# Third tiles of an attention and FFN kernel in Strassen pairs, with the attention pieces re-placed around them

## The chip, the cores and the metric

The kernel runs on one NeuronCore of a Trainium2 chip. The metric is the time of one execution on the device in microseconds; of the kernel before three executions are shown (242.56, 241.81 and 242.93 us) and their median, 242.56 us, is the time before.

The core has five instruction streams that run at once and meet at semaphores. TensorE (PE in the profile) multiplies matrices into PSUM. VectorE (DVE), ScalarE (ACT) and GpSimd (POOL) work on elements. SyncE (SP) mostly issues transfers. Each stream runs in the order in which the program was written, so an instruction that waits holds up all that stand behind it on its engine.

## The reference, cut to what matters

Attention over 4 batches, 8 heads, 768 positions and head dimension 64 is followed by a gated FFN over all 3072 tokens.

```python
scores = scale * np.matmul(q, k.transpose(0, 1, 3, 2))
keep = is_global | is_local            # first 8 positions, or the last 96
scores = np.where(keep, scores - slopes * dist, -1e9)
a = softmax(scores)
x = np.matmul(a, v)                    # heads side by side: [3072, 512]
out = (np.maximum(x @ w_gate, 0) * (x @ w_val)) @ w_out      # 512 -> 1536 -> 512
```

Keys that count are a band of 96 positions and the 8 global ones, so scores are needed in narrow spans only.

## The kernel before

**Halves and stages.** The work is cut into eight halves of a batch (`NHALF`), 384 tokens each. Half c passes through attention, which leaves a normalised and transposed `xT` of 4 chunks of 128 by 384, and then through the FFN. The main loop (L834 on) runs one stage per half c from 2 to 7: the FFN of half c, with the attention of half c + 1 and the preparation of q and k of half c + 2 strewn among it. Halves 0 and 1 and the first weights are handled by an order written out by hand before the loop. In this text stage c begins at the first gate matmul of half c.

**FFN of a half** (`ffn_pieces`, L509). For each of 12 blocks of 128 hidden columns, `gate` (L521) does four matmuls of 384 columns into a PSUM bank and a relu on ScalarE; `val` (L528) does four more and a product on VectorE that reads the bank and writes the block of `ht`. Then `ht` (1536 hidden values by 384 tokens) is multiplied with `w_out`. The 384 tokens are three tiles of 128. A plain tile (`outp`, L533) is 12 matmuls of 512 columns in four parts of three, a copy on ScalarE and a store. From half 1 on, tiles 0 and 1 go as a pair by Strassen's scheme: hidden index, output columns and token tiles are each split in two, and seven products `p1` to `p7` (L595 to L629, via `block` at L579) of six matmuls with 256 columns replace eight. The sums of weight blocks (`bs`) are made once, at L805. The sums of `ht` blocks are made on VectorE for each half: `sum_cb`, `sum_ad`, `sum_de` (L566 to L576), parts of them right behind some val blocks (`behind`), three parts after the last. p1, p3 and p4 are copied from PSUM by ScalarE; p2 and p5 are each read by two VectorE combinations, p6 and p7 by one each, and p6 and p7 add onto the banks in which p3 and p1 were made, which are so held from p3 and p1 to the end. The order on TensorE is p4, p3, p1, p2, p5, p6, p7, after the plain third tile.

**Attention of a half** (`attention_pieces`, L493) is 26 small pieces over four pairs of heads. Each pair has three QK pieces (`piece_qk`, L408: the first makes the scores of both steps in four PSUM banks and the exps of step 0, the second the exps of step 1 and the masks of step 0, the third the masks of step 1), two AV pieces (`piece_av`, L416: value matmuls, ln on ScalarE, and at the second also the reciprocal by exp) and a norm (`piece_norm`, L443: two VectorE products, which write `xT`). The masks (`masks`, L349) multiply the exps by a table `m_all` of decays, one instruction per span: step 0 of an odd half has three spans (432, 144 and 96 elements), of an even half two (432 and 48).

**Preparation** (`early_pieces`, L377): eight casts of q and k on POOL, three DMA transposes on SP, and four pieces that bring the keys into order (`piece_order`, L372; copies into `kT` on POOL).

**The order.** `spread` (L659) gives pieces places as shares of a stage, `weave` (L664) puts each piece behind the first FFN item that reaches its place. An FFN item counts 0.65 per block or product, so a stage counts 22.75: 15.6 of gate and val blocks, 2.6 of the plain tile and 4.55 of products. Attention is spread over 0 to 0.8 (0.07 to 0.82 in stage 2), preparation over 0.25 to 0.75. A half's loads are issued at a stage's start.

**PSUM.** In the loop three banks (`ff`) serve gate, val, the plain tile and p4, p3, p1, p6, p7, and five (`x`) scores, AV, p2 and p5. A new tile takes a bank that is free or becomes free first in the planner's order, and waits for the last reader of the tile before.

**SBUF** pools that matter: `setupp` and `efp` close with the early part, and the pools of the late part (`late`, `osb` with three buffers for output rows, `sums`) are laid in their place. `dd` is the table of distances from which the masks are made.

Of the kernel before, what the change touches and what calls it, by code (L numbers as in the profile page):

```python
# [8 lines left out]
FP32 = mybir.dt.float32  # L9
BF16 = mybir.dt.bfloat16  # L10
AF = mybir.ActivationFunctionType
ALU = mybir.AluOpType
# [3 lines left out]
def kernel(  # L16
# [12 lines left out]
    nc = tc.nc  # L29
# [67 lines left out]
    dd = const.tile([128, 2, NN, WQ], BF16)  # L97
# [75 lines left out]
    kq0 = firstp.tile([128, 2, H, NN * D], FP32, name="kq0")  # L173
    kq1 = setupp.tile([128, 2, H, NN * D], BF16, name="kq1")
# [173 lines left out]

    def masks(s, p, g, steps=steps_of):  # L349
        for j in steps[s % 2][g]:  # L350
# [157 lines left out]

    def ffn_pieces(c):  # L509
# [43 lines left out]

        N2, D2 = N_FC // 2, DM // 2
        tiles_ = [slice(n * 128, (n + 1) * 128) for n in range(2)]

        def sums_of(name, *shape):
            if name not in st:
                st[name] = late["sums"].tile([128, *shape], BF16, name=name)
            return st[name]  # L560

        cb = lambda: sums_of("cb", N2, 2, 128)
        ad = lambda: sums_of("ad", N2, 128)
        de = lambda: sums_of("de", N_FC, 128)

        def sum_cb(i0, i1):  # L566
            nc.vector.tensor_tensor(cb()[:, i0:i1].rearrange("f i n t -> f i (n t)"), ht[:, i0:i1, 0:256],
                                    ht[:, N2 + i0 : N2 + i1, 0:256], op=ALU.add)

        def sum_ad(i0, i1):  # L570
            nc.vector.tensor_tensor(ad()[:, i0:i1], ht[:, i0:i1, tiles_[0]],
                                    ht[:, N2 + i0 : N2 + i1, tiles_[1]], op=ALU.add)

        def sum_de(i0, i1):
            x, y = (1, 0) if i0 < N2 else (0, 1)
            nc.vector.tensor_tensor(de()[:, i0:i1], ht[:, i0:i1, tiles_[x]], ht[:, i0:i1, tiles_[y]],  # L576
                                    op=ALU.subtract)

        def block(key, pool, left, right, start, stop):  # L579
            if start:  # L580
                st[key] = psum[pool].tile([128, 512], FP32, name=f"{pool}_ps")
            for i in range(N2):
                nc.tensor.matmul(st[key][:, 0:D2], lhsT=left(i), rhs=right(i),  # L583
                                 start=start and i == 0, stop=stop and i == N2 - 1,
                                 skip_group_check=not start)
            return st[key][:, 0:D2]

        c0, c1 = slice(0, D2), slice(D2, DM)
        bs = lambda name: lambda i: late["bs"][name][:, i]
        V2 = nc.vector.tensor_tensor  # L590

        def store(n, cols, eng=nc.sync):
            eng.dma_start(out=out_v[c, n][:, cols], in_=st["r", n][:, cols])

        def p4():  # L595
            for n in range(2):
                st["r", n] = late["osb"].tile([128, DM], FP32, name="osb")
            ps = block("d", "ff", lambda i: ht[:, N2 + i, tiles_[1]], bs("b21-b11"), True, True)
            nc.scalar.copy(st["r", 0][:, c0], ps)

        def p3():
            ps = block("c", "ff", lambda i: ht[:, i, tiles_[0]], bs("b12-b22"), True, True)
            nc.scalar.copy(st["r", 0][:, c1], ps)

        def p1():
            ps = block("a", "ff", lambda i: ad()[:, i], bs("b11+b22"), True, True)
            nc.scalar.copy(st["r", 1][:, c1], ps)
# [6 lines left out]
        def p5():  # L614
# [3 lines left out]
            if c == NHALF - 1:  # L618
                store(1, c0)
                store(0, c1)  # L620
# [258 lines left out]
```

## Time and profile before

| what | value |
|---|---|
| median of three executions | 242.56 us |
| the profiled execution | 241.74 us |
| its span, first to last instruction | 239.9 us |
| mean granted TensorE clock | 0.998 |
| TensorE busy | 233.5 us, 97% |
| VectorE busy | 173.3 us, 72% |
| ScalarE busy | 153.4 us, 64% |
| GpSimd busy | 85.9 us, 36% |
| stages 3, 4, 5, 6 | 26.91, 27.67, 27.02, 27.47 us |
| stage 7, to the last combination's start | 22.8 us |

How to read it: the span is what the program's instructions cover; the execution's own time is 1.8 us longer. A matmul's listed duration reaches past the start of the next one, so the cost of a run of matmuls is taken from start to start; the same holds, with a tenth of a microsecond, on VectorE and ScalarE. An idle time in brackets carries the engine whose signal came last. Idle time on an engine that nobody waits for costs nothing.

### The profile page before, as it was taken

To read this page: it belongs to the slowest core of one execution; us is meant where nothing else is said; L and a number is where in the kernel's file an instruction comes from. 1 tells how busy PE (TensorE), PEld (TensorE's weight loads), DVE (VectorE), ACT (ScalarE), POOL (GpSimd) and SP (SyncE) were. 2 spreads that over 40 slices of the span, in tenths; PEclk is the share of its full clock that TensorE was granted. 3 is DMA by queue.
4 is the path that set the end of the run, shared out by engine and by line. 5 is a ranking of instruction groups with operands and counts; after the bars stand their busy time and mean duration, and the time that the engine had idled before them with its cause. 6 is when DMAs were issued, how large, how long until landed. Compare 5 with 4: busy or idle time off the path is not lost.

```text
span 239.9 us, 5355 instructions
## 1 busy us (share of the span) xinstructions
PE 233.5 (97%) x1937; PEld 146.6 (61%) x1945; DVE 173.3 (72%) x456; ACT 153.4 (64%) x347; POOL 85.9 (36%) x202
## 2 busy tenths in 40 slices
PE   7899999999999999999999999999999999999994
PEld 3655555665458566666668566676658566676663
DVE  7775955869677788777787687866887677764643
ACT  5897883337775777748774777638774677733330
POOL 6767893208414860903274060902350000000000
PEclk9999999999999999999999999999999999999999
DMA  6999999993976997098519939398431200030003
GB/s 200 181 198 177 257 234 219 185 162 61 270 178 134 301 150 131 8 185 257 108 25 122 285 93 133 19 166 262 67 68 44 90 0 0 3 129 3 4 27 104
DMA packets 69603, 31.42 MB, mean 131 GB/s; under 512 B 47160, under 2 KB 66616, under 8 KB 69576
## 3 DMA queue, kind: packets, MB, share of 16 engines
q0 software_dynamic: 31744, 8.71, 35.3%
q1 hardware_dynamic: 36616, 21.45, 35.1%
q10 hardware_dynamic: 1216, 0.92, 1.2%
q8 instruction: 15, 0.25, 0.4%
q14 instruction: 12, 0.10, 0.1%
HBM read 28.41 MB, written 6.29 MB: 145 GB/s over the span
## 4 chain that ended last, share of the span: by engine, by line
PE 91%; ACT 3%; DVE 2%; issue 1%; ACTq 0%
PE ff_ps L518 53%; PE ff_ps L538 9%; PE ff_ps L583 8%; PE x_ps L427 6%; PE x_ps L397 4%; PE x_ps L583 3%; PE t_ps L459 2%; PE s_ps L341 2%; PE t_ps L272 1%; PE t_ps L682 1%; ACT lnd L436 1%; PE t_ps L310 1%; DVE xT L446 1%; PE s_ps L321 1%; ACT rcp L441 0%
## 5 line engine op out<-in xcount | busy, mean ns | idle before, releaser
L518 PE MATMUL ff_ps<-xT,wg 128*128 128x384 bf16 x384 | 80.7, 326 | 0.5 <-ACT grelu L525 0.4
L518 PE MATMUL ff_ps<-xT,wv 128*128 128x384 bf16 x384 | 80.2, 326 | 0.0
L531 DVE TENSOR_TENSOR ht<-ff_ps,grelu 128x384 bf16<-128x384 f32 x96 | 53.1, 554 | 28.5 <-PE ff_ps L518 13.8
L525 ACT ACTIVATE grelu<-ff_ps 128x384 bf16<-128x384 f32 x96 | 47.1, 492 | 39.4 <-PE ff_ps L518 20.9
L518 PEld LDWEIGHTS <-wg 128*128 128x128 bf16 x384 | 35.9, 98 | 23.9 <-issue 0.9
L518 PEld LDWEIGHTS <-wv 128*128 128x128 bf16 x384 | 36.1, 97 | 23.4 <-issue 1.2
L406 ACT ACTIVATE es<-x_ps 128x360 bf16<-128x360 f32 (+2 forms) x96 | 36.8, 444 | 16.9 <-PE x_ps L397 16.8
L359 DVE TENSOR_TENSOR es<-es,m_all 128x432 bf16<-128x432 bf16 (+4 forms) x108 | 31.2, 334 | 8.2 <-ACT es L406 7.8
L446 DVE TENSOR_TENSOR xT<-x_ps,rcp 64x384 bf16<-64x384 f32 x48 | 26.6, 554 | 9.4 <-ACT rcp L441 8.8
L436 ACT ACTIVATE lnd<-x_ps 64x384 f32<-64x384 f32 x48 | 23.3, 485 | 12.5 <-PE x_ps L427 11.8
L538 PE MATMUL ff_ps<-wo_sb,ht 128*128 128x512 bf16 x112 | 29.6, 379 | 0.4
L363 POOL CAST kqc<-ks 128x384 bf16<-128x384 f32 x24 | 11.6, 532 | 32.3 <-DMA ks<-in_k_dram 32.3
L137 POOL DMA_DIRECT2D vbuf<-in_v_dram x25 | 21.6, 880 | 2.6 <-DMA wv<-in_moe_w_val_dram 2.1
L427 PE MATMUL x_ps<-es,vbuf 128*128 128x216 bf16 (+4 forms) x216 | 21.8, 225 | 0.0
L427 PEld LDWEIGHTS <-vbuf 128*128 128x128 bf16 x216 | 15.8, 97 | 7.7
L538 PEld LDWEIGHTS <-ht 128*128 128x128 bf16 x120 | 10.8, 97 | 9.8 <-issue 0.2
L263 POOL COPY kT<-kqT 128x240 bf16<-128x240 bf16 x16 | 6.9, 430 | 23.0 <-DMA kqT<-kqc 20.5
L363 POOL CAST kqc<-qs 128x384 bf16<-128x384 f32 x24 | 11.6, 522 | 8.1 <-DMA qs<-in_q_dram 8.1
L259 POOL COPY kT<-kqT 128x360 bf16<-128x360 bf16 x10 | 6.0, 604 | 19.9 <-DMA kqT<-kqc 19.9
L441 ACT ACTIVATE rcp<-lnd 128x384 f32<-128x384 f32 x24 | 12.6, 524 | 0.7
L347 ACT ACTIVATE ef<-s_ps 128x720 bf16<-128x720 f32 (+2 forms) x16 | 10.9, 710 | 2.1 <-PE s_ps L341 1.8
L397 PE MATMUL x_ps<-kqT,kT 64*128 64x216 bf16 (+4 forms) x216 | 11.8, 224 | 0.2
(115 smaller groups left out, 252.8 us busy)
## 6 DMA issues: line engine op xcount, KB each, us to landing
out_dram<-osb SPq DMA_DIRECT2D x22, 256.0 KB, 2.7
ks<-in_k_dram SPq DMA_DIRECT2D x6, 768.0 KB, 5.5
qs<-in_q_dram SPq DMA_DIRECT2D x6, 768.0 KB, 12.1
vbuf<-in_v_dram POOLq DMA_DIRECT2D x21, 120.0 KB, 7.9
wg<-in_moe_w_gate_dram POOLq DMA_DIRECT2D x3, 512.0 KB, 7.9
wv<-in_moe_w_val_dram POOLq DMA_DIRECT2D x3, 512.0 KB, 9.8
wo_sb<-in_moe_w_out_dram POOLq DMA_DIRECT2D x1, 1536.0 KB, 19.6
kq<-in_q_dram ACTq DMA_DIRECT2D x2, 192.0 KB, 4.7
```

What stands on the lines that cost most here:

```text
L137: nc.gpsimd.dma_start(out=v_dst(b, NG + r0, NG + r0 + n, j), in_=v[b, :, KT * j + r0 : KT * j + r0 + n, :].rearrange("h p d -> p h d"))
L359: nc.vector.tensor_mul(for_all, for_all, mk)
L363: nc.gpsimd.tensor_copy(kqc[:, :, i].rearrange("t n (h d) -> t h n d", d=D)[:, 2 * p : 2 * p + 2], of[s][:, 2 * p : 2 * p + 2, :].rearrang ...
L406: nc.scalar.activation(es[:, e, 0:c], banks[e][:, 0:c], AF.Exp, bias=0.0, scale=scale)
L427: nc.tensor.matmul(av3[:, :, a : a + w], lhsT=vb[:, j, z0 : z0 + 128], rhs=es[:, e, c : c + NN * w].rearrange("k (n p) -> k n p", n=NN), s ...
L436: nc.scalar.activation(ln[o0 : o0 + 64], av[d0 : d0 + 64, 0:QH], AF.Ln, bias=0.0, scale=1.0)
L446: nc.vector.tensor_tensor(xT_of[s][r, p, :], av_of[s, p, e][r, 0:QH], av_of[s, p, "r"][r], op=ALU.mult)
L518: nc.tensor.matmul(st[key][:, 0:QH], lhsT=w_of(w, dc, fc), rhs=xT_of[c][:, dc, :], start=(dc == 0), stop=(dc == N_DC - 1))
L525: nc.scalar.activation(gr, psg[:, 0:QH], AF.Relu, bias=0.0, scale=1.0)
L531: nc.vector.tensor_tensor(ht[:, fc, :], psv[:, 0:QH], st["gr", fc], op=ALU.mult)
L538: nc.tensor.matmul(ps2, lhsT=ht[:, fc, n * 128 : (n + 1) * 128], rhs=wo_sb[:, fc, :], start=(fc == 0), stop=(fc == N_FC - 1))
L583: nc.tensor.matmul(st[key][:, 0:D2], lhsT=left(i), rhs=right(i), start=start and i == 0, stop=stop and i == N2 - 1, skip_group_check=not s ...
```

## The change

Four things are changed together.

1. In halves 4 and 5, and in 6 and 7 (`PAIRED`), the two third tiles no longer go as plain tiles: half 5 multiplies its own third tile and that of half 4 as a second Strassen pair (`products3`), and half 7 those of 7 and 6. The Strassen code becomes a function `strassen` of any two tiles. Halves 4 and 6 so have only their own pair behind the last val block, with p3 ahead of p4 and p4 in an `x` bank (`bare`); halves 5 and 7 have two pairs in a row. `ht` of the earlier half is kept until the pair is done. The sums of the second pair are made in halves 5 and 7, three behind val blocks 1, 6 and 7 and two after the last.
2. The first three attention pieces (scores, exps and masks of the first pair of heads) of halves 5 and 7 move a stage forward, to between the products of halves 3 and 5 (places 0.82 to 0.93 and 0.885 to 0.975).
3. In stages 4 and 6 the last AV piece and the last norms have fixed places (0.76 and 0.84), behind the last val block and behind the sums and p1; the other pieces are spread over 0.07 to 0.735.
4. The masks of step 0, for halves from 3 on, are copied once on POOL into a table without gaps (`pack_mask`, five copies, between the casts and the ordering copies of half 2), and one VectorE instruction per pair of heads uses them instead of three or two.

Beside these, output rows have four buffers instead of three, and `dd` moves to the pool of the early part.

```diff
-    dd = const.tile([128, 2, NN, WQ], BF16)
+    dd = setupp.tile([128, 2, NN, WQ], BF16, name="dd")
...
+    def pack_mask(half, i):
+        todo = [by[half, j] for j in steps_later[half][0]]
+        if half not in packed_of:
+            packed_of[half] = late["packed"].tile([128, H, sum(NN * t[2] for t in todo)], BF16, name=f"packed{half}")
+        c = sum(NN * t[2] for t in todo[:i])
+        j, _, w, m = todo[i]
+        nc.gpsimd.tensor_copy(
+            packed_of[half][:, :, c : c + NN * w].rearrange("k h (n t) -> k h n t", n=NN),
+            m_all[:, :, 0 if j == 0 else 1, :, m : m + w])
...
     def masks(s, p, g, steps=steps_of):
+        if s > 2 and g == 0:
+            mk = packed_of[s % 2][:, 2 * p : 2 * p + 2]
+            es = es_of[s, p, steps[s % 2][0][0]][0][:, :, 0 : mk.shape[2]]
+            nc.vector.tensor_mul(es, es, mk)
+            return
...
+    def strassen(pair, sums, bare=False):
...
+        def p4():
+            ps = block("d", "x" if bare else "ff", lambda i: h(1, N2 + i, N2 + i + 1)[:, 0], bs("b21-b11"), True, True)
+            nc.scalar.copy(rows(0)[:, c0], ps)
...
+        return sum_cb, sum_cb_of, sum_ad, sum_de, [(0.65, f) for f in (((p3, p4) if bare else (p4, p3)) + (p1, p2, p5, p6, p7))]
...
+    PAIRED = (4, 6)
+    third_of = {}
...
+        plain = range(NN) if c < 1 else () if c - c % 2 in PAIRED else (NN - 1,)
+        sum_cb, _, sum_ad, sum_de, products = strassen([(c, ht, 0), (c, ht, 1)], "sums", c in PAIRED)
...
+        rest = (lambda: sum_ad(3, 6), lambda: sum_cb(3, 6), lambda: sum_de(9, 12))
+        if c in PAIRED:
+            third_of[c] = ht
+        elif c - 1 in PAIRED:
+            _, cb3, ad3, de3, products3 = strassen([(c, ht, NN - 1), (c - 1, third_of[c - 1], NN - 1)], "sums3")
+            behind[1] = [lambda: cb3(1)]
+            behind[6] = [lambda: ad3(0, N_FC // 2)]
+            behind[7] = [lambda: de3(0, N_FC // 2)]
+            rest = (lambda: cb3(0), lambda: de3(N_FC // 2, N_FC)) + rest
...
+            f2 += (products3 if c - 1 in PAIRED else []) + products
+            places = (2, 3, 5) if plain else (0, 1, 2) if c in PAIRED else (0, 1, 2, 3, 4)
+            for at, f in list(zip(places, rest))[::-1]:
                 f2.insert(at, (0.0, f))
...
-    late["osb"] = ctx.enter_context(tc.tile_pool(name="osb", bufs=3, reuse_waits="tile"))
+    late["osb"] = ctx.enter_context(tc.tile_pool(name="osb", bufs=4, reuse_waits="tile"))
...
+    packs = [lambda half=half, i=i: pack_mask(half, i) for half, i in ((1, 0), (1, 1), (1, 2), (0, 0), (0, 1))]
...
-              casts[7], *xs, lambda: spread_v_globals(1), *order_k[:2]):
+              casts[7], *xs, lambda: spread_v_globals(1), *packs, *order_k[:2]):
...
+        if c + 1 < NHALF:
+            pieces = ahead.pop(c + 1, None) or attention_pieces(c + 1)
+            if c in PAIRED:
+                placed.append([(0.76, pieces[-2][1]), (0.84, pieces[-1][1])])
+                placed.append(spread(pieces[:-2], 0.07, 0.735))
+            else:
+                placed.append(spread(pieces, *(0.07, 0.82) if c == 2 else (0.0, 0.8)))
+        if c + 1 in PAIRED:
+            ahead[c + 2] = attention_pieces(c + 2)
+            placed.append(spread([ahead[c + 2].pop(0) for _ in range(3)], *(0.885, 0.975) if c - 1 in PAIRED else (0.82, 0.93)))
```

The seven products and their combinations are those of the code before, with tile 0 and tile 1 replaced by the two tiles of the pair (`h(0, ...)` and `h(1, ...)`). With the changed counts stages 4 and 6 count 20.15 items' worth and stages 5 and 7 24.7.

## The prediction

> **What bounds the kernel now.** I read the page first: engine shares and the chain that ended last.
>
> ```profile
> span 239.9 us, 5355 instructions
> PE 233.5 (97%) x1937; PEld 146.6 (61%) x1945; DVE 173.3 (72%) x456; ACT 153.4 (64%) x347; POOL 85.9 (36%) x202
> PE 91%; ACT 3%; DVE 2%; issue 1%; ACTq 0%
> ```
>
> TensorE is busy for 97% of the span and 91% of the last chain is its own. So a change is worth the TensorE time it removes, less the new waits. Then I cut the trace into stages, one per half c, at the first gate matmul of each (start:end length, then busy time per engine).
>
> ```profile
> 104.78:131.69 26.91, 26.86 (x214) 17.45 (x214) 20.01 (x51) 18.34 (x44) 11.28 (x25) 1.00 0.71 134
> 131.69:159.36 27.67, 27.56 (x232) 17.85 (x230) 21.47 (x54) 18.98 (x44) 9.93 (x23) 1.00 0.72 132
> 159.36:186.38 27.02, 26.97 (x214) 17.45 (x214) 20.56 (x50) 18.34 (x44) 7.26 (x20) 1.00 0.47 118
> 186.38:213.85 27.47, 27.40 (x232) 17.84 (x231) 20.41 (x54) 18.98 (x44) 0.00 (x0) 1.00 0.08 30
> ```
>
> These are stages 3 to 6. TensorE has under 0.2 us of idle time in each; VectorE has 6 to 7 us, but not everywhere. Third, the timeline of the last stage prices both ways to multiply a tile: the plain third tile, then p4 and p3, then p1.
>
> ```profile
> 229.28 2.75 PE L538 MATMUL ff_ps<-wo_sb,ht 128*128 128x512 bf16 x11
> 231.88 1.47 PE L583 MATMUL ff_ps<-bs,ht 128*128 128x256 bf16 x12
> 233.19 0.82 PE L583 MATMUL ff_ps<-bs,ad 128*128 128x256 bf16 x6
> ```
>
> Start to start, the plain tile's 12 matmuls (one record is missing) take 2.60 us, 217 ns each, and 12 products' matmuls 1.31 us, 109 ns each. Last, VectorE at the end of stage 5: two sums, the last norms, a sum, the first combination.
>
> ```profile
> 181.02 0.36 DVE L571 TENSOR_TENSOR ad<-ht 128x384 bf16<-128x384 bf16 x1
> 181.30 0.55 DVE L567 TENSOR_TENSOR cb<-ht 128x768 bf16<-128x768 bf16 x1
> 182.25 1.12 DVE L446 TENSOR_TENSOR xT<-x_ps,rcp 64x384 bf16<-64x384 f32 x2 [0.41 <-ACT rcp L441]
> 183.39 0.36 DVE L576 TENSOR_TENSOR de<-ht 128x384 bf16<-128x384 bf16 x1
> 184.51 0.42 DVE L611 TENSOR_TENSOR osb<-x_ps,osb 128x256 f32<-128x256 f32 x1 [0.76 <-ACT osb L607]
> ```
>
> Prices, start to start: a sum of 384 elements 0.28, of 768 0.48, a pair of norms 1.14, a combination 0.33 (184.51, 184.85, 185.18). A val product takes 0.59 when the next instruction reads it (174.60 to 175.19).
>
> **The change, part by part.**
>
> *The pairs.* Each removes two plain tiles, 2 x 2.60 = 5.20 us, and adds 42 matmuls of 256 columns, 42 x 0.1093 = 4.59. That is 0.61 a pair, **-1.22 us** for two, all on TensorE. A rule speaks against this. The Trainium skill ("TensorE: Matmul & The Clock Gate", Back-to-back issue gap) gives sustained spacings of about 81 ns at 128 columns and 131 ns at 512; interpolated, an estimate of 98 ns at 256, and a pair would cost 42 x 0.098 - 24 x 0.131 = 1.0 us more instead of 0.6 less, +1.9 for both. The rows show 217 and 109, nearly proportional to columns, and decide.
>
> On VectorE stages 5 and 7 gain five sums of 768 elements (2.4 us) and six combinations (2.0 us). On ScalarE three copies of 0.37 replace two of 0.57, 0.0 net. ScalarE has 8 us idle per stage. Stage 7 has no attention; its VectorE is busy 12.1 of 26 us, so the extra work is covered.
>
> *Masks packed.* An odd half's first mask step is now 432+144+96 elements in three instructions, 0.56 us (133.78 to 134.34). One of 672, between the sums of 384 and 768, is 0.42: 0.14 x 4 off VectorE per odd half, some 0.1 x 4 per even half. TensorE doesn't wait on it except for one attention block: five value matmuls at 152.51 held it 0.50 instead of 0.30, four at 179.68 0.39 instead of 0.28. In the new order these blocks lie further behind their masks: **-0.3**, bounds -0.3 and 0.
>
> *Packing copies.* Five copies on POOL, 4608 elements. The copies of kT give 0.36 us between starts for 240 elements and 0.48 for 360, so 1.0 ns an element and 0.12 fixed: 5.2 us, put between the last cast and the first ordering copy.
>
> ```profile
> 47.17 0.50 POOL L363 CAST kqc<-qs 128x384 bf16<-128x384 f32 x1
> 54.78 0.74 POOL L259 COPY kT<-kqT 128x360 bf16<-128x360 bf16 x1 [7.12 <-DMA kqT<-kqc]
> ```
>
> POOL waits there for 7.12 us for the transposes, so I cost the copies at nothing. Behind them on POOL's queue are the keys of half 2 (needed by TensorE at 57.23, there at 55.96, 1.3 us of slack), the markers that let SP load half 3's q and k (57.2), and half 3's v; its first keys are in order at 76.4, its scores come at 79.19. Without the cover they'd cost the excess over 8.4 us. The other side: masks beside a POOL copy took 0.93 instead of 0.60 (151.96). At that half speed the wo sum at 51.38 ends 0.6 late and the val product behind it at 53.0; its PSUM bank is wanted at 53.23. So 0. The Trainium skill ("SBUF — State Buffer", SBUF: two separate sides) says that a GpSimd instruction and a VectorE one with two SBUF inputs exclude each other for a whole instruction. Then that sum would wait until about 52.5 and TensorE would lose an estimated 0.4 us (a sum of +0.5 instead of +0.1). The row's slowdown of half is milder.
>
> *Earlier scores.* They add no work: 0.51 us of TensorE moves from stage 4 into 3, and from 6 into 5. At 134.0 and 188.69 TensorE waits 0.19 and 0.18 for a relu behind the first exps; with these gone from there, **-0.37**, bounds -0.4 and 0. Half 5's keys are ordered by 124.75, wanted at 128.3; half 7's have 5 us. Half 6's come within the shorter stage 4: in order at 150.4, wanted about 158. No DMA is moved; on SP's queue the three stores of a half become two in halves 4 and 6 and four in 5 and 7, still behind the half's transposes and ahead of the next loads.
>
> *dd in the early pool, a fourth osb buffer:* space only, 0. dd's last reader (the masks) ends some 20 us before that space is reused.
>
> *New waits, end of stage 3.* p3 ends at 128.25; scores to 128.76; p7 then ends at 132.04. ScalarE's four exps delay p1's copy to 130.0 and the second exps to 130.8. VectorE: p2's combinations 130.3 to 131.0, masks to 131.5, p5's to 132.17, p6's to 132.55. The next stage's first val product takes p6's bank and is due at 132.37: **+0.25** with a restart. Bounds 0 to 0.5.
>
> *End of stages 4 and 6.* No plain tile follows val 11 (zero at its end on TensorE). The attention pieces crowd: AV of pair 2 puts its ln and rcp ahead of relu 10 on ScalarE, so VectorE runs val 10 1.0 before zero, then a sum and norms (1.14), and val 11 only at 1.05 to 1.61. p4 starts at 0.96 and its sixth matmul wants val 11 at 1.5: 0.15. The sums end at 2.66, the last norms, put behind them, at 3.80; then six combinations, p6's ending at 5.56, while the next stage's first val is due at 5.37: 0.25. **+0.4 each**, bounds 0 to 0.8.
>
> *End of stage 5*, zero as before. VectorE's queue: val 11 at 0.27, then 0.59, sums 0.48 and 0.48, masks 0.57, sum 0.28, norms 1.14, sum 0.48, two combinations 0.67, sum 0.28, two 0.67 and the pair's p6 0.33, at 6.24; last norms 1.14; its p7 at 7.75. TensorE: three attention blocks of 0.28 and seven products of 0.655 end at 5.43, p4 of the next pair at 6.08. Its p3 wants the bank of the first pair's p6, at 6.30: 0.25. Its p1 gets p4's bank, which ScalarE frees at 6.7, and doesn't wait. After p2 the scores of half 7 take four of five x banks and p2 holds the fifth, so p5, ready 0.51 after p2, waits until an exp or two combinations free one, 0.95 after it: 0.45, with p6, p7 and the next stage's gate queued behind it on TensorE. Then masks and combinations queue into stage 6: 0.2. **+0.9**, bounds 0.45 (the x bank; no reason removes it) to 1.7 (p1 must take the first p7's bank, at 7.8).
>
> *Sum:* -1.22 -0.30 -0.37 +0.25 +0.40 +0.90 +0.40 = **+0.06 us**. The profiled execution took 241.74 (span 239.9 and 1.8 around it), 0.82 below the median of 242.56 that the change is compared with. So 242.56 + 0.06: **242.6**, no difference: 0.5% (1.2 us) is about what a measurement of this kernel can tell from no change.
>
> **The rivals.**
>
> *The waits don't come* (faster). If VectorE catches up in the tails, as before (it idles 0.76 ahead of the first combination at 184.51), only the x bank's 0.45 is left: -1.89 + 0.45 = -1.44, **241.1**. For it: bounds of 0 in three places. Against it: the removed 2.60 us covered just these sums, and stage 5's queue fills 7.5 us with no gap.
>
> *VectorE bounds stage 5's end* (slower, near the bound). p1 waits until 7.8: +0.8, and the stage-6 end takes its upper bound, +0.4 more: **243.8**. For it: three ff banks, of which two are held for whole pairs. Against it: p4's bank is free 1.1 us earlier.
>
> *POOL's packing runs over* (slower). In the trace, beside dense VectorE work, the kT copy of 360 took 0.74 and 0.86: 1.9 to 2.25 ns an element, 9.4 to 11.0 us for all five. From 47.67 that ends at 57.1 to 58.7, the first keys 1.2 later, and TensorE stands 1.1 to 2.7: with the sum, **244.6** at 2.0. It decides from 8.4 us of copying on. Against it: between 47.7 and 51.4 VectorE does only val products, 0.56 in each 1.3 us.
>
> **How the numbers follow.** No difference 0.47, waits don't come 0.25, VectorE bounds 0.18, packing 0.10. Faster: 0.25 and 0.02 of the forecast's lower edge, 0.27. Slower: 0.10, half of 0.18 and 0.03 of the upper edge, 0.22. Same: 0.51. The forecast's own range is 241.6 to 243.6 (its bounds together, as independent errors). For 8 in 10 it reaches to the faster rival, 241.0, and past the VectorE rival, 244.0; left out are the packing case and half a tenth on either side.
>
> **What would show it.** Right: no 512-column matmuls in stages 4 to 7, 84 more of 256 columns at 109 ns; stage 3 27.7 us, stage 4 24.5, stage 5 30.2, stage 6 24.5, stage 7 24.8 to its last matmul (22.8 before); POOL's five copies 5 to 7 us before 54.8; TensorE idle ahead of half 7's p5. Wrong: TensorE gapless at these stage ends, or late ahead of 57.23, or products slower than 109 ns.

## The result, and the profile after

The changed kernel takes 243.22 us (median of 14 runs, 242.74 to 244.57), the kernel before, run beside it, 241.76 us (14 runs, 240.86 to 242.93). The ratio is 1.0072, with a 95% interval of 1.0056 to 1.0088: 1.7 us slower (1.46 between the two medians). The predicted 242.6 us and its range hold the time, but the forecast behind them, no difference, does not stand: by the 0.5% named there this is a slowdown. That the time came within 0.6 of 242.6 is in part luck. The prediction counted from 242.56, the median of three executions, and 14 executions put the kernel before at 241.76. Counted from there, its +0.06 would have given 241.8.

The profiled execution of the changed kernel took 244.09 us, of which 242.3 are the span; it is 0.87 above the median. The page answers to the lines shown of before:

```profile
span 242.3 us, 5435 instructions
PE 233.5 (96%) x1977; PEld 149.9 (62%) x1981; DVE 182.1 (75%) x446; ACT 153.2 (63%) x349; POOL 92.4 (38%) x207
PE 81%; DVE 9%; ACT 4%; issue 3%; DMA 1%; ACTq 0%; DVEq 0%
```

VectorE (DVE) is busy 8.8 us longer (173.3 before), GpSimd (POOL) 6.5. In the chain that ended last TensorE's share falls from 91% to 81% and VectorE's rises from 2% to 9%: TensorE now waits for VectorE. The same stages as before, 3 to 7, from one first gate matmul to the next (start:end length, then PE, PEld, DVE, ACT, POOL busy; the prediction cut the stages of before one matmul later, 0.16 to 0.17 us, which leaves their lengths as they are to 0.01):

```profile
106.08:133.51 27.43, 27.38 (x226) 17.64 (x225) 20.69 (x49) 19.77 (x48) 11.46 (x25) 1.00 0.73 135
133.51:158.43 24.92, 24.64 (x211) 16.27 (x208) 19.83 (x43) 16.88 (x39) 10.00 (x23) 1.00 0.52 124
158.43:189.53 31.10, 29.80 (x257) 20.64 (x255) 25.34 (x61) 20.29 (x50) 8.70 (x21) 1.00 0.55 120
189.53:213.86 24.33, 24.33 (x210) 16.36 (x208) 19.12 (x46) 16.88 (x39) 0.00 (x0) 1.00 0.06 23
213.86:238.87 25.01, 24.93 (x182) 17.50 (x179) 16.57 (x39) 8.11 (x18) 0.00 (x0) 1.00 0.13 48
```

Compare length and PE busy in each row: the difference is TensorE's idle time, 0.28 us in stage 4 and 1.30 in stage 5, where it was 0.11 and 0.05. The wait for a stage's first val product lies behind the cut, so it counts in the next stage. Cut in this way, the prediction's terms and the profiles give (us; the last stage to the end of its last matmul, not counting how far its listed time reaches past the next start):

| stage | 3 | 4 | 5 | 6 | 7 | sum |
|---|---|---|---|---|---|---|
| before | 26.92 | 27.67 | 27.02 | 27.47 | 22.77 | 131.85 |
| predicted | 27.43 | 24.57 | 30.37 | 24.53 | 25.01 | 131.91 |
| after | 27.43 | 24.92 | 31.10 | 24.33 | 25.01 | 132.79 |

The row "predicted" is worked out afterwards from the terms. The prediction's own list, 27.7, 24.5, 30.2, 24.5 and 24.8, counts the wait at the end of stage 3 in stage 3 and is rounder elsewhere. By the row, stages 3 and 7 came as predicted; stage 4 is 0.35 too long, stage 5 0.73, stage 6 0.20 shorter. That makes the 0.9 us which these stages lose. The rest lies ahead of stage 3, which begins at 106.08 instead of 104.61: 1.47 us in the profiled executions. The two profiles are level up to the first sum of w_out's quarters (51.37 and 51.38 us), so this is lost behind it. The profiled execution is 0.87 above its median, so this second loss may be smaller in most executions. There are two losses to explain.

**Ahead of stage 3: the packing.** From the timeline of the changed kernel (start, length, engine, line; idle time before and what ended it in brackets):

```profile
49.07 4.54 POOL L358 COPY packed<-m_all 128x1728 bf16<-128x1728 bf16 x5
...
50.89 0.56 DVE L649 TENSOR_TENSOR ht<-ff_ps,grelu 128x384 bf16<-128x384 f32 x1 [0.74 <-PE ff_ps L636]
...
51.37 2.65 DVE L862 TENSOR_TENSOR bs<-wo_sb 128x768 bf16<-128x768 bf16 x1
...
53.94 0.55 DVE L649 TENSOR_TENSOR ht<-ff_ps,grelu 128x384 bf16<-128x384 f32 x1
54.40 0.54 DVE L862 TENSOR_TENSOR bs<-wo_sb 128x768 bf16<-128x768 bf16 x1
54.53 0.32 PE L636 MATMUL ff_ps<-xT,wg 128*128 128x384 bf16 x1 [1.15 <-DVE ht L649]
```

The five packing copies run back to back from 49.07 to 53.61. VectorE's sum of w_out's quarters (L862) starts at 51.37 and takes 2.65 us, where it takes 0.54 at 54.40: it ends 0.4 after the last copy. The val product queued behind it starts at 53.94, and TensorE, whose PSUM bank that product frees, stands for 1.15 us. The val product at 50.89, which reads PSUM, ran beside the same copies in its usual 0.56.

**Stage 4's end: the key copies.** The same view, at the end of stage 4:

```profile
152.48 0.53 POOL L259 COPY kT<-kqT 128x360 bf16<-128x360 bf16 x1 [6.14 <-DMA kqT<-kqc]
152.52 0.71 DVE L564 TENSOR_TENSOR de<-ht 128x384 bf16<-128x384 bf16 x1
...
154.29 0.56 DVE L649 TENSOR_TENSOR ht<-ff_ps,grelu 128x384 bf16<-128x384 f32 x1
...
154.91 0.28 PE L570 MATMUL x_ps<-bs,ht 128*128 128x256 bf16 x1 [0.22 <-DVE ht L649]
154.99 0.66 POOL L259 COPY kT<-kqT 128x360 bf16<-128x360 bf16 x1
...
155.18 0.89 DVE L553 TENSOR_TENSOR cb<-ht 128x768 bf16<-128x768 bf16 x1
...
155.60 0.53 POOL L260 COPY kT<-kqT 128x24 bf16<-128x24 bf16 x1
...
155.99 0.35 DVE L564 TENSOR_TENSOR de<-ht 128x384 bf16<-128x384 bf16 x1
...
159.23 0.48 PE L636 MATMUL ff_ps<-xT,wv 128*128 128x384 bf16 x2 [0.32 <-DVE osb L613]
```

A sum of 384 elements took 0.71 at 152.52 and 0.35 at 155.99; one of 768 took 0.89, and 0.55 elsewhere. The long ones lie beside the copies that put half 6's keys in order, and the two engines take turns: the sum at 155.18 ends 0.42 after the copy of 154.99 does (155.65), and the copy of 24 elements at 155.60, 0.20 where it stands alone, ends when the sum does, to 0.06. In the kernel before the same copies began at 149.48, 17.95 us into the stage, and met masks (0.93 for 0.60) and one sum (0.55 for 0.35) that no product was held up by. They begin when the transposed keys land, 18.97 us into the changed stage; that stage is 2.75 us shorter, so they now meet the sums that its products wait for. Val 11 comes late for the sixth matmul of p4 (p1 starts 0.39 us late by it), the sum of 768 late for p2 (0.12), and the combinations late for the next stage's val product.

**Stage 5's end.** VectorE and TensorE from the same view:

```profile
179.73 0.84 DVE L377 TENSOR_TENSOR es<-es,m_all 128x432 bf16<-128x432 bf16 x2
...
184.18 0.42 DVE L613 TENSOR_TENSOR osb<-ff_ps,osb 128x256 f32<-128x256 f32 x1
...
184.65 0.81 PE L570 MATMUL ff_ps<-bs,ht 128*128 128x256 bf16 x6 [0.60 <-DVE osb L613]
185.30 0.82 PE L570 MATMUL ff_ps<-bs,ad 128*128 128x256 bf16 x6
...
187.56 0.81 PE L570 MATMUL x_ps<-wo_sb,cb 128*128 128x256 bf16 x6 [0.38 <-ACT es L424]
```

The masks at 179.73 took 0.84, beside the ordering of half 7's keys (177.7 to 181.7 on GpSimd): 0.76 to the next instruction, where 0.57 was predicted. The sums on either side of them hold VectorE 0.07 longer each, and p6's combination, at 184.18, ends 6.77 after the last gate and val products (177.83) where 6.24 was predicted. The second pair's p3 waits 0.60 for that bank, 0.77 with the restart, instead of 0.25. p1 (185.30) follows without a wait. p5 waits 0.38 for an x bank, 0.44 with the restart, as predicted.

### The profile page after: what moved, and what is told of

It reads as the page before. It is cut to its first block, busy times and chain, and to the rows that moved or that the text cites. A ratio compares the mean times of both kernels' runs of the same rounds, so it can differ in the third digit from the quotient of the medians.

```text
span 242.3 us, 5435 instructions
## 1 busy us (share of the span) xinstructions
PE 233.5 (96%) x1977; PEld 149.9 (62%) x1981; DVE 182.1 (75%) x446; ACT 153.2 (63%) x349; POOL 92.4 (38%) x207
## 4 chain that ended last, share of the span: by engine, by line
PE 81%; DVE 9%; ACT 4%; issue 3%; DMA 1%; ACTq 0%; DVEq 0%
PE ff_ps L636 51%; PE ff_ps L570 7%; PE x_ps L445 5%; PE ff_ps L656 5%; PE x_ps L415 4%; PE x_ps L570 3%; DVE xT L464 2%; PE t_ps L477 2%; PE s_ps L341 2%; PE t_ps L272 2%; ACT lnd L454 1%; PE t_ps L733 1%; PE t_ps L310 1%; DMA out_dram<-osb 1%; DVE ht L649 1%
## 5 line engine op out<-in xcount | busy, mean ns | idle before, releaser
L636 PEld LDWEIGHTS <-wv 128*128 128x128 bf16 x384 | 35.9, 97 | 24.8 <-issue 2.0
L636 PEld LDWEIGHTS <-wg 128*128 128x128 bf16 x384 | 36.0, 97 | 24.5 <-issue 2.5
L424 ACT ACTIVATE es<-x_ps 128x360 bf16<-128x360 f32 (+2 forms) x96 | 36.2, 446 | 10.7 <-PE x_ps L415 10.7
L136 POOL DMA_DIRECT2D vbuf<-in_v_dram x25 | 21.6, 875 | 2.5 <-DMA wv<-in_moe_w_val_dram 1.6
L377 DVE TENSOR_TENSOR es<-es,m_all 128x432 bf16<-128x432 bf16 (+4 forms) x56 | 18.3, 368 | 2.1 <-ACT es L424 2.0
L656 PE MATMUL ff_ps<-wo_sb,ht 128*128 128x512 bf16 x68 | 17.8, 379 | 0.2
L381 POOL CAST kqc<-qs 128x384 bf16<-128x384 f32 x24 | 12.5, 558 | 11.6 <-DMA qs<-in_q_dram 11.6
L570 PE MATMUL x_ps<-wo_sb,cb 128*128 128x256 bf16 x108 | 13.7, 273 | 0.4 <-ACT es L424 0.4
L570 PE MATMUL ff_ps<-bs,de 128*128 128x256 bf16 x108 | 13.3, 272 | 0.0
L564 DVE TENSOR_TENSOR de<-ht 128x384 bf16<-128x384 bf16 (+1 forms) x32 | 12.8, 400 | 0.5
L366 DVE TENSOR_TENSOR es<-es,packed 128x672 bf16<-128x672 bf16 (+1 forms) x20 | 10.4, 519 | 3.4 <-ACT es L424 3.4
```

Source lines behind the costliest of these rows:

```text
L136: nc.gpsimd.dma_start(out=v_dst(b, NG + r0, NG + r0 + n, j), in_=v[b, :, KT * j + r0 : KT * j + r0 + n, :].rearrange("h p d -> p h d"))
L377: nc.vector.tensor_mul(for_all, for_all, mk)
L381: nc.gpsimd.tensor_copy(kqc[:, :, i].rearrange("t n (h d) -> t h n d", d=D)[:, 2 * p : 2 * p + 2], of[s][:, 2 * p : 2 * p + 2, :].rearrang ...
L424: nc.scalar.activation(es[:, e, 0:c], banks[e][:, 0:c], AF.Exp, bias=0.0, scale=scale)
L636: nc.tensor.matmul(st[key][:, 0:QH], lhsT=w_of(w, dc, fc), rhs=xT_of[c][:, dc, :], start=(dc == 0), stop=(dc == N_DC - 1))
L656: nc.tensor.matmul(ps2, lhsT=ht[:, fc, n * 128 : (n + 1) * 128], rhs=wo_sb[:, fc, :], start=(fc == 0), stop=(fc == N_FC - 1))
```

## The experiments

The theory was: the pairs, the early scores and the banks do what the prediction says; the two losses are GpSimd copies that hold VectorE's sums, in the packing and at the ends of stages 4 and 5. The rivals were that the new order itself overloads VectorE, that the early scores cost more than they give, and that the half pairs' banks do. Each run is given with its ratio to the kernel before, run on the same chip, and with the stages that bear on it. The diff has one more edit that the section on the change does not list: within a stage the loads and the preparation now stand ahead of the attention in the list that is woven in. No run takes it alone; the run with the one pair of halves 6 and 7 has it too, and its stages 3 and 4 are no longer than before.

**Packing taken out of the changed kernel.**

```
 def masks(s, p, g, steps=steps_of):
-        if s > 2 and g == 0:
+        if False:
...
-              casts[7], *xs, lambda: spread_v_globals(1), *packs, *order_k[:2]):
+              casts[7], *xs, lambda: spread_v_globals(1), *order_k[:2]):
```

> The changed kernel without the five packing copies; masks are applied span by span as before. Theory (POOL's packing copies hold VectorE up, in the profiled execution a sum of 0.55 us took 2.65 and TensorE stood 1.15 + 0.17): TensorE runs through 50 to 58 us without a gap and the time falls by 0.4 to 1.4 us (less or more as the w_out load releases the copies early or late), to 241.8 to 242.8. Rival (the loss lies in the stage ends alone): 243.2 within 0.3.

Measured: 242.50 against 241.43 us, ratio 1.0045 (1.0031 to 1.0058). Stages 27.43, 24.77, 31.09, 24.47, 25.00, sum 132.76: as in the changed kernel, so packed masks buy TensorE nothing there, and the AV blocks are as short with separate masks. TensorE has no wait between 45 and 60 us: the stall is gone. (Stage 3 begins at 105.71 in this profile all the same, because its work before the first sum, at 52.39, ran a microsecond later; in the profiles without packing that start lies between 104.08 and 105.71.) By the ratios the packing costs 0.27%, 0.65 us, give or take 0.5, since each ratio has an interval of about 0.14% to either side.

**Packing alone, in the kernel before.** The helper, the packed first step of the masks and the five copies, and nothing else.

```
+        if s > 2 and g == 0:
+            mk = packed_of[s % 2][:, 2 * p : 2 * p + 2]
...
+            nc.vector.tensor_mul(es, es, mk)
+            return
...
-              casts[7], *xs, lambda: spread_v_globals(1), *order_k[:2]):
+              casts[7], *xs, lambda: spread_v_globals(1), *packs, *order_k[:2]):
```

> The kernel before with the packed masks alone. Theory (packing copies hold VectorE up): slower than before by 0.3 to 1.4 us with a gap on TensorE between 52 and 58 us, less 0.2 for shorter masks. Rival (the loss lies in the stage ends): equal to before or up to 0.3 faster.

Measured: 242.61 us, ratio 1.0049 (1.0033 to 1.0065), 1.2 us, while stages 3 to 7 are 0.14 shorter. Its timeline:

```profile
49.58 4.53 POOL L358 COPY packed<-m_all 128x1728 bf16<-128x1728 bf16 x5
...
51.38 3.14 DVE L828 TENSOR_TENSOR bs<-wo_sb 128x768 bf16<-128x768 bf16 x1
...
55.04 0.81 PE L536 MATMUL ff_ps<-xT,wg 128*128 128x384 bf16 x4 [1.64 <-DVE ht L549]
```

The copies started 0.51 later than in the changed kernel and ended at 54.11; the sum began at the same time, ended at 54.52, again 0.4 after them, and took 3.14. So it is not slowed in a proportion; it stands until the run of copies is over. The packing costs 0.65 us in one comparison and 1.2 in the other, which the intervals do not tell apart. There is a reason for which it may vary, though. The copies start when w_out has landed; a small copy marks that moment (before, then changed):

```profile
47.04 0.18 POOL L819 COPY held<-wo_sb 1x1 bf16<-1x1 bf16 x1 [4.32 <-DMA wo_sb<-in_moe_w_out_dram]
...
48.49 0.18 POOL L873 COPY held<-wo_sb 1x1 bf16<-1x1 bf16 x1 [1.88 <-DMA wo_sb<-in_moe_w_out_dram]
```

The packing does not cause the later landing: in the run above, without any packing, the marker stands at 50.00. What counts is the time from the marker to the first sum, since the sum waits for the end of the copies. It is 2.88 us in the changed kernel, 2.38 with packing alone, and 2.39 to 4.34 in the ten profiles without packing, where the kernel before has the longest. How much the loss varies with it from execution to execution was not measured.

**The packing kept, the sums of w_out's quarters later** (changed kernel).

```
-                 0.1, 0.74))
+                 0.21, 0.8))
```

> The changed kernel, packing kept, with the sums of w_out blocks spread from 0.21 to 0.8 instead of 0.1 to 0.74, so that the first comes some 2.7 us later, behind the packing copies. Theory (it is the meeting of the copies with a VectorE sum of two SBUF inputs that costs): as without packing or up to 0.3 faster, 241.6 to 242.7, and no instruction on VectorE of over 1.2 us. Rival (POOL's copies delay the keys, or cost by themselves): 243.2 within 0.3.

Measured: 242.16 us, ratio 1.0033 (1.0018 to 1.0048). The same copies, and the first such sum behind them:

```profile
49.19 4.54 POOL L358 COPY packed<-m_all 128x1728 bf16<-128x1728 bf16 x5
...
55.03 0.55 DVE L862 TENSOR_TENSOR bs<-wo_sb 128x768 bf16<-128x768 bf16 x1
```

With no sum of two SBUF tiles issued during the copies, the copies cost no stall, and the ratio agrees with that of the run without packing: 4.5 us of GpSimd are hidden, as the prediction had it; what was not hidden is the meeting.

**The key copies of halves 6 and 7 left out** (changed kernel without the packing; those two halves' scores are made with older keys).

```
 def piece_order(s, p):
+        if s >= 6:
+            return
```

> The changed kernel without packing, and with the ordering copies of the keys of halves 6 and 7 on POOL left out (their scores are then made with older keys: that part of the computation is changed). Theory (these copies fall on the stage ends and hold VectorE's sums up): stage 4 falls by 0.2 to 0.4 us and stage 5 by 0.4 to 0.7, 0.6 to 1.1 us in all below the kernel without packing. Rival (VectorE's own work fills the stage ends): within 0.2 us of it.

Measured: 241.43 against 241.55 us, ratio 0.9994 (0.9983 to 1.0004). Stage 4 is 24.44, stage 5 30.42, together 1.0 us less than with the copies; the other stages are unchanged. At the two places shown above:

```profile
150.53 0.35 DVE L566 TENSOR_TENSOR de<-ht 128x384 bf16<-128x384 bf16 x1
...
152.81 0.55 DVE L555 TENSOR_TENSOR cb<-ht 128x768 bf16<-128x768 bf16 x1
...
176.91 0.59 DVE L377 TENSOR_TENSOR es<-es,m_all 128x432 bf16<-128x432 bf16 x2
...
181.49 0.81 PE L572 MATMUL ff_ps<-bs,ht 128*128 128x256 bf16 x6 [0.17 <-DVE osb L615]
```

Sums and masks are back at 0.35, 0.55 and 0.59, and p3's wait is 0.17, 0.33 with the restart. Stages 4 and 5 now stand 0.13 below and 0.05 above the prediction. So for stages 3 to 7 the prediction's sum holds for a VectorE that meets no key copies there, and the meeting is the second loss.

**Keys in order, but moved away from the sums** (changed kernel without the packing): half 6's on ScalarE, and half 7's pairs 1 to 3 written behind stage 5's products.

```
-        copy = nc.scalar.copy if s == 2 and p >= 2 else nc.gpsimd.tensor_copy
+        copy = nc.scalar.copy if s == 2 and p >= 2 or s == 6 else nc.gpsimd.tensor_copy
...
-        out += [(0.0, lambda p=p: piece_order(s, p)) for p in range(HP)]
+        out += [(0.0, lambda p=p: piece_order(s, p)) for p in range({6: 0, 7: 1}.get(s, HP))]
...
         weave(f1 + f2, *placed)
+        for p in range({4: 0, 5: 1}.get(c, HP), HP):
+            piece_order(c + 2, p)
```

> The changed kernel without the packing (e1), with all keys ordered, but not beside the sums: half 6's on ScalarE behind stage 4's last product, half 7's pairs 1 to 3 on GpSimd at the start of stage 6. If the meeting of key copies and sums is what costs the 1.1 us that e5 took away, stages 4 and 5 come near e5's 24.4 and 30.4 and the ratio near 1.000 to 1.001; ScalarE's idle 4 us at the start of stage 5 take 12 copies of 0.2 to 0.4 us, so the first relu and exps of stage 5 may be some 0.2 late. Rival: e5 was faster because its scores of halves 6 and 7 did not wait for new keys; then this one stays at e1's ratio of 1.0045 or goes above it.

Measured: 242.04 against 241.46 us, ratio 1.0026 (1.001 to 1.0041). Stage 4 is 24.43, as with no copies at all: the rival, that the run above was fast because scores did not wait for new keys, falls for half 6. For half 7 no run tests it, but in the changed kernel its keys are in order at 181.74 and its first scores run at 186.71, so these did not wait for them. Stage 5 is 30.86, halfway, and what it gained belongs to the first move: its first val product waits 0.24 instead of 0.48, while p3 waits 0.60 as before. The second move did nothing, and its timeline shows why:

```profile
176.68 0.55 POOL L265 COPY kT<-kqT 128x48 bf16<-128x48 bf16 x1
177.18 0.74 POOL L263 COPY kT<-kqT 128x240 bf16<-128x240 bf16 x1
...
177.57 0.89 DVE L377 TENSOR_TENSOR es<-es,m_all 128x432 bf16<-128x432 bf16 x2
```

GpSimd had been idle for 5.98 us, and took the first of the copies at 174.33, when the keys landed. The program writes them behind stage 5's last product, which TensorE starts at 186.7: the later place in the program did not delay them, because GpSimd had nothing else to do. The masks met them again, 0.89.

**Half 7's first scores behind the second pair's p3** (changed kernel without the packing), so that p5 finds an x bank.

```
-            placed.append(spread([ahead[c + 2].pop(0) for _ in range(3)], *(0.885, 0.975) if c - 1 in PAIRED else (0.82, 0.93)))
+            placed.append(spread([ahead[c + 2].pop(0) for _ in range(3)], *(0.845, 0.96) if c - 1 in PAIRED else (0.82, 0.93)))
```

> As the kernel without packing copies, and in stage 5 the first scores of half 7 go behind p3 instead of p2 (places 0.845 to 0.96). Theory (p5 waits 0.44 us because the scores and p2 hold all five x banks): 0.3 to 0.5 us faster than without packing alone, p5 waits for nothing. Rival (VectorE is the bound there, so the wait only moves to another product): within 0.15 of it.

Measured: 242.63 us, ratio 1.005 (1.0029 to 1.0071). Stage 5 is 30.55, 0.54 shorter, stage 6 25.05, 0.58 longer. p3's wait stays and the other one moved:

```profile
182.37 0.81 PE L570 MATMUL ff_ps<-bs,ht 128*128 128x256 bf16 x6 [0.71 <-DVE osb L613]
...
187.97 0.48 PE L636 MATMUL ff_ps<-xT,wv 128*128 128x384 bf16 x2 [0.67 <-DVE osb L613]
```

p5 no longer waits, and the next stage's val product now waits 0.67 for VectorE's combinations instead. The rival held: the x bank is where the wait shows, VectorE is what sets the end of stage 5.

**Stage 5's attention earlier** (changed kernel without the packing), to empty VectorE ahead of the two pairs.

```
-                placed.append(spread(pieces, *(0.07, 0.82) if c == 2 else (0.0, 0.8)))
+                placed.append(spread(pieces, *(0.07, 0.82) if c == 2 else (0.0, 0.7) if c == 5 else (0.0, 0.8)))
```

> The changed kernel without packing, with the attention of half 6 spread over 0 to 0.7 of stage 5 instead of 0.8, so that its masks and norms come before the two pairs. Theory (VectorE's queue at the end of stage 5 makes the waits of the second pair's p3 and p5): the wait ahead of p3, 0.7 us, goes; stage 5 falls by 0.5 to 0.9 us. Rival (it stands there for the POOL copies or the banks, whatever the order): within 0.2 us.

Measured: 243.74 us, ratio 1.0088 (1.007 to 1.0105); stage 5 is 32.01, 0.92 longer. TensorE's waits in that stage:

```profile
160.18 0.81 PE L636 MATMUL ff_ps<-xT,wv 128*128 128x384 bf16 x4 [0.58 <-ACT grelu L643]
...
183.62 0.81 PE L570 MATMUL ff_ps<-bs,ht 128*128 128x256 bf16 x6 [0.46 <-ACT osb L588]
186.80 0.82 PE L570 MATMUL x_ps<-wo_sb,cb 128*128 128x256 bf16 x6 [0.38 <-ACT es L424]
```

This idea fell. The denser exps put a relu 0.58 late, and p3 waits for a bank all the same, now one that ScalarE copies. Work that is pulled ahead in a full stage is paid for there.

**The early scores undone** (changed kernel without the packing).

```
-                placed.append(spread(pieces[:-2], 0.07, 0.735))
+                placed.append(spread(pieces[:-2], 0.0, 0.735))
...
-        if c + 1 in PAIRED:
+        if False:
```

> The changed kernel without packing and with all attention pieces of halves 5 and 7 in their own stages 4 and 6, as before the change (the last two keep their fixed places). By the prediction's terms the early scores were worth -0.37 at the stage starts and cost +0.25 at the end of stage 3 and +0.65 at that of stage 5, so 0.5 us faster than without packing alone. Rival (stages 4 and 6 are too short for all 26 pieces, VectorE falls behind there): 0.3 us or more slower.

Measured: 243.78 us, ratio 1.0091 (1.0074 to 1.0107). Stages 3 to 7 are 26.91, 26.11, 29.88, 25.95, 25.00: stages 4 and 6 gain 1.34 and 1.48, stages 3 and 5 lose 0.52 and 1.21. The relu at the start of stage 4:

```profile
134.99 0.81 PE L636 MATMUL ff_ps<-xT,wv 128*128 128x384 bf16 x4 [0.75 <-ACT grelu L643]
```

There TensorE waits 0.75 for the relu behind the first exps, and as long in stage 6, not the 0.19 and 0.18 of the kernel before. So beside the pairs the early scores are worth 1.1 us, three times what the prediction gave them: the attention of a stage without a plain tile is squeezed into less time, and its first exps come closer.

**The early scores alone, in the kernel before.**

```
+            pieces = ahead.pop(c + 1, None) or attention_pieces(c + 1)
+            first_ = 0.07 if c in (2, 4, 6) else 0.0
+            placed.append(spread(pieces, first_, 0.82 if c == 2 else 0.8))
+        if c + 1 in (4, 6):
+            ahead[c + 2] = attention_pieces(c + 2)
+            placed.append(spread([ahead[c + 2].pop(0) for _ in range(3)], 0.82, 0.93))
```

> The kernel before with the early scores of halves 5 and 7 alone (places 0.82 to 0.93 of stages 3 and 5, the rest of their pieces from 0.07 on). By the prediction's terms: -0.37 at the stage starts, +0.25 at each of two stage ends, so +0.1, within 0.3 of before. Rival (the relu waits that they remove were hidden anyway): 0.4 to 0.8 us slower.

Measured: 241.93 us, ratio 1.0018 (1.0006 to 1.003). Stages 27.42, 27.23, 27.42, 27.21, 22.78, sum 132.06, 0.21 over before; 0.4 by the ratio. Without the pairs they are no gain: they repay only what the pairs squeeze.

**One pair each.** The changed kernel without the packing, with the pair of halves 6 and 7 alone, and with that of halves 4 and 5 alone.

```
-    PAIRED = (4, 6)
+    PAIRED = (6,)
```

> The changed kernel without the packing (e1), with one pair only: halves 6 and 7; halves 4 and 5 have their plain third tiles as before, and only half 7's first scores are a stage sooner. My theory: what the two pairs lose is lost at the ends of the stages in which VectorE has attention work as well; stage 7 has none, and at the end of stage 6 no key copies run on GpSimd. So stages 3 and 4 as before (26.9, 27.7 us), stage 5 27.4 (the scores moved into it, as in e8), stage 6 24.4 to 24.5 and stage 7 25.0: a sum of 131.4 for stages 3 to 7 against 131.85, so 0.4 us under the kernel before, a ratio of 0.998. Rival: a pair costs VectorE the same wherever it stands; then half of e1's loss, a ratio of 1.002.

```
-    PAIRED = (4, 6)
+    PAIRED = (4,)
```

> The changed kernel without the packing (e1), with one pair only: halves 4 and 5; halves 6 and 7 as before. My theory: this pair is the costly one, since stage 5 has its own attention work and the sums of stage 4 meet the key copies: stages 3 to 5 as in e1 or, with half 7's first scores no longer moved into stage 5, 0.4 shorter there (27.4, 24.8, 30.7), stages 6 and 7 as before (27.5, 22.8), a sum of 133.1 against 131.85: a ratio of 1.005. Rival: both pairs cost the same, a ratio of 1.002.

Measured, against 241.46 us: with halves 6 and 7 alone 241.06 us (11 runs), ratio 0.9981 (0.9972 to 0.999); with halves 4 and 5 alone 242.57 us (6 runs), ratio 1.0046 (1.0029 to 1.0062). Stages 3 to 7 of the first:

```profile
104.39:131.30 26.91, 26.86 (x216) 17.45 (x215) 20.38 (x51) 18.34 (x44) 11.41 (x25) 1.00 0.71 135
131.30:158.76 27.46, 27.39 (x231) 17.85 (x230) 21.31 (x55) 18.98 (x44) 10.35 (x23) 1.00 0.58 127
158.76:186.27 27.51, 27.46 (x226) 17.64 (x225) 21.29 (x55) 19.77 (x48) 7.77 (x20) 1.00 0.51 121
186.27:210.71 24.44, 24.38 (x211) 16.37 (x209) 19.03 (x50) 16.88 (x39) 0.00 (x0) 1.00 0.06 23
210.71:235.71 25.00, 24.93 (x182) 17.50 (x179) 16.55 (x39) 8.11 (x18) 0.00 (x0) 1.00 0.13 48
```

No stage has more than 0.07 us of idle TensorE. The sum is 131.32, 0.53 under before. Not all of that is the pair: 0.21 lie in stage 4, which has none. There one block of value matmuls is shorter (before, then this run; 0.50 and 0.31 from start to start):

```profile
152.51 0.67 PE L427 MATMUL x_ps<-es,vbuf 128*128 128x216 bf16 x5
...
152.27 0.47 PE L445 MATMUL x_ps<-es,vbuf 128*128 128x216 bf16 x5
```

TensorE and VectorE run that stage in the order of before. What differs is that the masks ahead of the block took 0.93 beside the key copies in the profile of before, and 0.62 here. Stages 5 to 7, where the pair is, are 0.31 shorter (76.95 for 77.26): about half of the 0.61 that a pair takes off TensorE, the rest being small waits such as 0.22 and 0.24 for the val products of stages 6 and 7. In the second, stages 3 to 5 are 27.44, 24.79, 30.54, and the sum is 133.01, 1.16 over before. So the pair of halves 6 and 7, whose second stage has no attention work and whose first has no GpSimd work (POOL 0.00), pays, and all the loss is the pair of halves 4 and 5. Not all of that is the key copies: without them both pairs together stood at 131.76, 0.09 under before, so the pair of halves 4 and 5 would still cost some 0.4 (0.53 less 0.09). That fits the waits for banks that the prediction had for stage 5, of which p3's 0.33 and p5's 0.44 are left in the run without key copies. The version with the one pair is the fastest of all: 0.4 us under the kernel before. That is less than the 0.5% taken as the bound of a difference; with 11 and 23 runs the interval lies below 1.

## Why the prediction was right or wrong

Right, by its steps:

- *The pairs, -1.22.* In stage 7 the pair's 42 products take 4.58 us, from 229.70 on TensorE's timeline to 234.28, 109.0 ns each; predicted 4.59. Its first group of products (p4 and p3), and the same group of the tiles behind it:

```profile
229.70 1.47 PE L570 MATMUL ff_ps<-bs,ht 128*128 128x256 bf16 x12
...
234.28 1.47 PE L570 MATMUL ff_ps<-bs,ht 128*128 128x256 bf16 x12
```

- *The relu waits, -0.37*, are gone from the starts of stages 4 and 6. As a value of the early scores the figure was too low, as the run without them shows, but the sum needed only the waits of before.
- *AV blocks, -0.30.* Those at 152.06 and 153.02 take 0.31 and 0.30 instead of 0.50, those at 177.83, 180.72 and 181.65 0.27 each instead of 0.39. The size is right; that the new order is the cause, as written, is not shown. The runs with packing alone and with the one pair of halves 6 and 7 keep the order of stage 4 and have the block at 0.31 as well. The 0.50 belongs to masks that took 0.93 beside the key copies in the profile of before (0.60 and 0.62 in those two runs), and the prediction took it for a cost that every execution of the kernel before has. So this term came out partly by luck.
- *End of stage 3, +0.25*: 0.23 was measured. Stage 6's end, +0.40, came to 0.27: p4 is 0.04 late and the val product 0.23.
- *p5's x bank, 0.45*: 0.44. *p1 doesn't wait*: it did not.
- *A packed mask of 672* was put between the sums of 384 and 768; it is 0.50 long, where those are 0.35 and 0.55. It bounds nothing.

Wrong:

- *Packing copies, 0.* The cover named, GpSimd's idle time, was there, and the copies' 4.54 us were even below the 5.2 estimated. Two things failed. The first is the price of a meeting, taken as a slowdown of half from masks beside a kT copy: the sum of w_out's quarters stood until the run of copies was over. The second is the start of the copies, 47.67 in the prediction, taken from one profile in which w_out landed early; in the changed kernel's profile they began at 49.07. The sum was to end 0.6 late, and ended 2.1 late in the changed kernel and 2.6 in the run with packing alone. Copies of 4.54 us from 47.67 would have ended at 52.21 and the sum, 0.41 behind them, at 52.6, an estimate of 0.7 late: at that start even the wrong price came out nearly right, and 0 would have held. The passage weighed a rule of the Trainium skill ("SBUF — State Buffer", SBUF: two separate sides) against that row and chose the row as the milder one. The rule is that a GpSimd instruction and a VectorE one with two SBUF inputs lock each other out for a whole instruction. The key copies above agree with it, sum and copy taking turns. At the packing the direction was right and the size was not: by the rule the sum of 51.37 would have waited for the copy that was running, which ended at 51.7, and it stood through two more. (The estimate of 52.5 from the rule went with copies from 47.67, so it is not to be set against the 54.02 at which the sum ended.) The packing rival was named with the wrong mechanism: GpSimd did not run over, nor did TensorE wait for the keys.
- *End of stage 4, +0.40.* Stage 4's excess of 0.35 (and part of stage 5's, whose first val product waits 0.47 with the restart instead of 0.25) comes from sums of 0.35 and 0.55 costed at their lone prices. The prediction asked only whether half 6's keys come in time, and not what their copies run beside. It also had them in order at 150.4, some 18.4 us into the stage, where the profile of before has 21.6 and the changed kernel 22.9 (156.43). The copies are tied to the landing of a load, so a shorter stage moves them against the sums.
- *End of stage 5, +0.90.* The same: masks at 0.76 instead of 0.57, two sums at 0.55 and 0.35 instead of 0.48 and 0.28, then p3's bank 0.77 instead of 0.25; without the key copies it is 0.33. The rival "VectorE bounds stage 5's end" had the engine right, as moving the scores shows, but not the place: the wait came at p3, on p6's bank, and not at p1.

With both meetings taken away, the run without the key copies stands at 0.9994 of before, -0.1 us where the sum of the terms was +0.06. So the error is these two meetings: by the ratios 0.65 us for the packing (1.0072 to 1.0045) and 1.2 for the key copies (1.0045 to 0.9994), each give or take 0.4 to 0.5. One slip in the range: the bounds, taken together as independent errors, give about 241.8 to 243.8 and not 241.6 to 243.6.

## What to carry to other kernels

Price a GpSimd copy by what VectorE does beside it, not by GpSimd's idle time: list every instruction of VectorE with two SBUF inputs that can fall into the copies' window, and, at the worst, take it as standing until the whole run of copies ends, as it did here beside long copies in a row. When a stage gets shorter, work that starts on a load's landing does not move with it; look at what it now stands beside. Do not take its moment, or a wait that goes with it, from one profile: in the profiles whose stage 4 has its plain tile, half 6's key copies began 17.35 to 19.07 us into it. And a change that buys TensorE time with VectorE work pays only in the stages where VectorE has room: here the same edit was worth -0.4 us in the last pair of halves and cost 1.1 in the pair before.

## What the runs showed that I had not expected

- A VectorE sum of two SBUF tiles that meets the back-to-back packing copies stands for the whole run, 2.65 and 3.14 us instead of 0.55, ending 0.41 us after the last copy in both cases. It does not go ahead between two copies, though there are boundaries while it stands. The single copies of the changed kernel, from a narrower cut of its timeline:

```profile
51.24 0.50 POOL L358 COPY packed<-m_all 128x384 bf16<-128x384 bf16 x1
...
51.70 1.62 POOL L358 COPY packed<-m_all 128x1728 bf16<-128x1728 bf16 x1
```

The sum, issued at 51.37, passes the boundaries at 51.7 and at 53.3. Val products, with one operand in PSUM, ran beside the same copies at 0.56.
- Beside the key copies the two engines take turns, so the loss is smaller: 0.35 to 0.71, 0.55 to 0.89, a pair of masks 0.59 to 0.84 and 0.89. GpSimd loses as well: a copy of 240 elements took 0.74 instead of 0.41. Nor does every meeting cost VectorE: with packing alone and with the one pair of halves 6 and 7, the pair of masks that took 0.93 in the profile of before took 0.60 and 0.62 while key copies ran, and it was copies that took longer (0.36 instead of 0.20, 0.63 instead of 0.53). Why VectorE gets in between these and not between the packing copies was not tried. The key copies have 24 to 360 elements, the packing copies 192 to 1728.
- Five GpSimd copies of 4608 elements in all took 4.54 us. From the two shown, (1.62 - 0.50) / (1728 - 384) is 0.83 ns an element, less than the 1.0 that the copies of kT had given.
